# Second forms of three x blocks made in gate/up and kept in DRAM

## The chip, the cores and the metric

The kernel runs on 1 core of one Trainium2 chip. The metric is the device time of one execution in microseconds, the median of several runs; lower is better.

## The reference

With x of 2048 rows and 512 columns, all in float32:

```
g   = sigmoid((x * gate_w).sum(-1))
a   = real(DFT_seq(DFT_hidden(x)))       # as matmuls with cos and sin matrices
h   = silu(x @ w1) * (x @ w3)            # 512 -> 1376, "gate" and "up"
b   = h @ w2                             # 1376 -> 512
out = g * a + (1 - g) * b
```

The DFT along the sequence comes first in the kernel (matrices times x), then the one along the hidden axis.

## The kernel before, in words

**Arithmetic.** Each float32 operand is split in two parts of type float32r: a high part, a rounded copy that ScalarE makes (`high`, line 108), and a low part, the difference, that VectorE makes (`low`, line 111). A product of two operands is three matmuls (`mm3`, line 122: high x high, high x low, low x high), each of 128 x 128 by 512 columns. On top of that, products of 2 x 2 blocks are made with seven multiplications instead of eight, so each operand is needed as seven *forms*: blocks and sums of blocks. "First forms" are four of them, made from sums over the raw block (`sums1_here`, lines 168 and 170), "second forms" the other three (`sum2`, line 174, and `forms2`).

**Stages.** 1. Gate/up: 22 items (numbers 0 to 21), each a block of 128 columns of w1 and w3 and one half of the rows of x. From item 1 on each item of the main loop is a call of `gate_up(n)`: seven products of six matmuls, in the order X, Z, a product for item n + 3, X, Z, another for n + 3, X. X and Z are two PSUM banks that are read by ScalarE or VectorE between the products that are added to them. From item 19 on there is nothing left for later items, and an item has five products. 2. Streamed products: nine blocks, numbers 0 to 3 over the DFT matrices (`cc`), then over h and over the result so far. A block consists of steps; in blocks 0 to 3 a step has 12 matmuls, and there are 28 steps: seven forms by four pieces. The streamed operand is loaded, summed (lines 682 and 685) and split (`zo`) three steps ahead; the standing operand is x (blocks 0 to 3), in first forms A1 (steps 0 to 15) and second forms A2 (steps 16 to 27).

**What is made in gate/up besides.** In items 9, 11, 13 and 15 a block of w2 is loaded, summed and split; its low halves are queued early in items 10, 12, 14 and 16, and its forms are stored to DRAM (`w2sp`, lines 568 and 571). In items 12, 14, 16, 17, 18, 19 and 20 a block of x (`xr`, loaded by `load_a`, line 578, 512 KB) is made into its first forms, the eighth block in item 21. The first forms stand in pool `a1`, which has eight places less one and fills up block by block; the pool takes the place of the first x operand of gate/up once item 11 is done.

**What sets the order.** The schedule is written by hand. Each engine takes its instructions in program order and waits at the first one that is not ready. The lists `early`, `ahead`, `second`, `mid` and `at_end` hold functions that `gate_up(n)` runs at five places between its products. In `gate_up`, the copy of X (line 369) comes before `early`; the copy of Z (line 373, ScalarE) comes after `ahead`; the addition of X (line 382, VectorE) comes after `second`. SP issues all loads in program order: in an item first `wb` (1 MB, the weights' second forms, from DRAM, from item 13 on) for the next item, then `ws` (raw weights) for four items on, whose split is `wa`, then what stands in the lists. POOL issues all stores in program order: two of h in each item (256 KB each), and w2's. The raw buffers (`wide`) rotate in the order in which they are freed, so that a load can wait for one.

**Second forms before.** In block 0, all eight x blocks are loaded again (`load_a2`, line 738, steps 4 to 11), and from step 7 on summed and split (`make_a2`), one block a step.

Of the kernel before, what the change touches and what calls it, by code (L numbers as in the profile page):

```python
# [7 lines left out]
F32 = mybir.dt.float32  # L8
F32R = mybir.dt.float32r
# [3 lines left out]
P = 128  # L13
# [8 lines left out]
NG = NST // 2  # L22
# [4 lines left out]
K = 9  # L27
W2_AT = (9, 11, 13, 15)
A1_AT = (12, 14, 16, 17, 18, 19, 20)


@with_exitstack
def fnet_swiglu_gate_kernel(
# [20 lines left out]
    nc = tc.nc  # L54

    def pool(name, bufs, side, space=None):
        kw = {} if space is None else {"space": space}
        cm = tc.tile_pool(name=name, bufs=bufs, side=side, reuse_waits="tile", **kw)
        return cm, cm.__enter__()
# [6 lines left out]
    dram = ctx.enter_context(tc.tile_pool(name="dram", bufs=1, space=bass.MemoryType.DRAM))  # L66
# [29 lines left out]
    def wide(name):  # L96
        return take(F4, [P, 1024], F32, name)
# [4 lines left out]
    def free(*tiles):  # L102
        for t in tiles:
            _, places, at = HELD.pop(id(t))
            places.append(at)

    def high(hi, src):
        nc.scalar.activation(hi, src, AF.Copy)  # L108

    def low(hi, lo, src):  # L110
        nc.vector.tensor_sub(lo, src, hi.bitcast(F32))  # L111

    def split(hi, lo, src):
        high(hi, src)
        low(hi, lo, src)
# [16 lines left out]
    gs = dram.tile([NTB, 1, 512], F32, tag="gs", name="gs")  # L132
    gsp, ngsp = (dram.tile([2, P, 1024], F32, tag=k, name=k) for k in ("gsp", "ngsp"))
    dsp = [dram.tile([KD, P, 2, n, 256], F32, tag=f"dsp{n}", name=f"dsp{n}") for n in (4, 3)]
    w2sp = [dram.tile([NP2, P, 2, n, 256], F32, tag=f"w2sp{n}", name=f"w2sp{n}") for n in (4, 3)]
    wbsp = dram.tile([NC, P, 2, 4, 256], F32, tag="wbsp", name="wbsp")
    zsp = dram.tile([4 * NTB * P, 1024], F32, tag="zsp", name="zsp")
# [3 lines left out]
    def flat(ap):  # L141
        return ap.rearrange("p a n -> p (a n)")
# [22 lines left out]
    def sums1_here(r):  # L165

        a21, a11, a12, a22 = (r[:, i * 256 : (i + 1) * 256] for i in range(4))
        nc.vector.tensor_sub(a22, a22, a21)
        for d, v, w in ((a21, a22, a11), (a12, a12, a21)):
            nc.vector.scalar_tensor_tensor(d, v, -1.0, w, op0=ALU.mult, op1=ALU.subtract)  # L170

    def sum2(r):

        nc.vector.tensor_sub(r[:, :256], r[:, 256:512], r[:, :256])

    def forms2(r, t2):

        r = r.rearrange("p (a n) -> p a n", a=4)
        split(flat(t2[:, 0, 0:2]), flat(t2[:, 1, 0:2]), flat(r[:, 2:4]))
        split(t2[:, 0, 2], t2[:, 1, 2], r[:, 0])  # L180
# [8 lines left out]
    NI = len(ITEMS)  # L189
# [149 lines left out]
    early, ahead, second, mid, at_end = {}, {}, {}, {}, {}  # L339
# [177 lines left out]
    def do(work, n, f, *a):  # L517
        work.setdefault(n, []).append(lambda: f(*a))
# [55 lines left out]
    A1, A2, XR = [], [], {}  # L574
# [13 lines left out]
    def low_a(p):  # L588
        low(*parts_a1(p))
        free(XR.pop(p))  # L590

    for n in range(NI):
        if n in W2_AT:
            p = W2_AT.index(n)
            do(at_end, n - 1, load_w2, p)
            do(early, n, sums_w2, p)
            do(mid, n, high_w2, p)
            do(early, n + 1, low_w2, p)
        if n in A1_AT:
            p = A1_AT.index(n)  # L600
            do(at_end, n - 1, load_a, p)
            do(early, n, lambda p=p: sums1_here(XR[p]))
            do(mid, n, high_a, p)
            do(early, n + 1, low_a, p)

# [4 lines left out]
    n = NI - 1 - LOOK  # L610
    do(at_end, n - 1, F4.extend, [(f4_a, f"f4_{k}") for k in range(4, 5 + LOOK)])
    for k in range(LOOK + 2):
        do(at_end, n - 1 + k, lambda k=k: load_c(k))
    do(at_end, NI - 2, load_a, NG - 1)
    do(early, NI - 1, lambda: sums1_here(XR[NG - 1]))
    do(mid, NI - 1, lambda: split_c(0))
# [38 lines left out]
    def block(blk, k, q):  # L655
        if KIND[blk] == "F":
            return cc[blk, ("B11", "B12", "B22", "B21").index(k), q]
        if KIND[blk] == "H":
            return hsp[blk - NTB, ("B11", "B12", "B21", "B22").index(k), q]
        return z_rows(2 * (blk - NTB - 2) + (k in ("B12", "B22")), 2 * (k in ("B21", "B22")) + q)  # L660

    def cols(blk, q, form):

        return 512 if KIND[blk] == "H" and q == NQ[blk] - 1 and form in ("B21", "B22", "T4") else 1024
# [38 lines left out]
    def load_c(m):  # L703
        while LOADS and LOADS[0][0] <= m and F4:
            _, blk, k, q = LOADS.pop(0)
            r = RAW[blk, k, q] = wide(f"{k}_{blk}_{q}")
            n = cols(blk, q, k)
            nc.sync.dma_start(r[:, :n], block(blk, k, q)[:, :n])
# [6 lines left out]
    for n in range(1, NI):  # L715
        gate_up(n)
        if ITEMS[n] == (NC - 1, 0):
            close(xo0_cm)
            a1_cm, a1 = pool("a1", 1, "left")
# [4 lines left out]
    a2_cm, a2 = pool("a2", 1, "right")  # L724
    ut_cm, ut = pool("ut", 1, "right")
    F4[:0] = [(f4_b, f"f4_{k}") for k in range(5 + LOOK, 13)]
    ZO[:0] = [(zo_b, f"zo_{k}") for k in range(2, 4)]
    def load_a2(p):


        if p < NG // 2:
            t = a2.tile([P, 2, 3, 256], F32, tag=f"a2_{p + NG // 2}", name=f"xs{p}")
            XR[p] = t.rearrange("p h a n -> p (h a n)")[:, :1024]
        elif p < NG - 2:
            XR[p] = flat(ut.tile([P, 2, 512], F32, tag=("u3", "c21")[p % 2], name=f"xs{p}"))
        else:
            XR[p] = wide(f"xs{p}")
        nc.sync.dma_start(XR[p], xn[p])

    def make_a2(p):  # L740
        A2.append(a2.tile([P, 2, 3, 256], F32R, tag=f"a2_{p}", name=f"a2_{p}"))
        r = XR.pop(p)
        forms2(r, A2[p])
        if p >= NG - 2:
            free(r)

# [199 lines left out]
    def at(blk, n, f, *a):  # L946
        todo.setdefault(START[blk] + n, []).append((f, a))

    at(1, 1, load_score, 1)
    for p in range(NG):  # L950
        at(0, 4 + p, load_a2, p)

        at(0, 7 + p, lambda p=p: sum2(XR[p]))
    for p in range(NG):
        at(0, 8 + p, make_a2, p)

    at(0, 0, lambda: nc.scalar.activation(act0, act0, AF.Sigmoid))
# [3 lines left out]
    for i, (src, sp, p) in enumerate(late):  # L961
        blk, b = 1 + i // 2, i % 2
        n = (17, 24)[b]
# [11 lines left out]
    for p in range(KD):  # L975
        early = p < NG - NP2
# [76 lines left out]
```

## Time and profile before

| | |
|---|---|
| median of 3 runs | 679.55 us (678.91 to 679.66) |
| the profiled execution: time, span | 679.73 us, 678.0 us |
| VectorE busy | 602.1 us |
| ScalarE busy | 366.9 us |
| HBM read, written | 114.82 MB, 57.16 MB |

In the rows, PE is TensorE, PEld its weight loads, DVE VectorE, ACT ScalarE, POOL GpSimd and SPq SyncE's DMA issues; q0 is the queue of POOL's transfers and q1 that of SP's. A row of a timeline gives start and length in us, engine, line, operation, what is written from what, shape and count; in brackets the idle time before it and what ended it. A row of the windows gives the stretch and its length, then busy us and instruction count of PE, PEld, DVE, ACT and POOL, the granted TensorE clock, the DMA share and GB/s. A row of the transfers gives size and us from issue to landing. The matmuls overlap, so the time from one to the next is read from starts, not from lengths. The clock was 1.00 throughout.

### The profile page before, as it was taken

To read this page: it belongs to the slowest core of one execution; us is meant where nothing else is said; L and a number is where in the kernel's file an instruction comes from. 1 tells how busy PE (TensorE), PEld (TensorE's weight loads), DVE (VectorE), ACT (ScalarE), POOL (GpSimd) and SP (SyncE) were. 2 spreads that over 40 slices of the span, in tenths; PEclk is the share of its full clock that TensorE was granted. 3 is DMA by queue.
4 is the path that set the end of the run, shared out by engine and by line. 5 is a ranking of instruction groups with operands and counts; after the bars stand their busy time and mean duration, and the time that the engine had idled before them with its cause. 6 is when DMAs were issued, how large, how long until landed. Compare 5 with 4: busy or idle time off the path is not lost.

```text
span 678.0 us, 8627 instructions
## 1 busy us (share of the span) xinstructions
PE 671.2 (99%) x3089; PEld 581.8 (86%) x3089; DVE 602.1 (89%) x737; ACT 366.9 (54%) x480; POOL 64.0 (9%) x118
## 2 busy tenths in 40 slices
PE   9999999999999999999999999999999999999997
PEld 6888888888888888888888888888888888888886
DVE  6999988787679999987999799979998897898996
ACT  6675566655446764464554554554546455445452
POOL 0011112121110000000110001100110000000000
PEclk9999999999999999999999999999999999999999
DMA  7585557499998656912497328915999982874942
GB/s 294 205 306 218 218 196 277 187 328 388 410 418 289 254 177 230 352 63 93 156 378 288 94 88 334 385 56 208 360 420 419 414 281 91 310 281 154 330 135 93
DMA packets 45547, 172.54 MB, mean 255 GB/s; under 512 B 5312, under 2 KB 5696, under 8 KB 41664
## 3 DMA queue, kind: packets, MB, share of 16 engines
q1 hardware_dynamic: 32608, 118.63, 48.2%
q0 software_dynamic: 12608, 52.97, 19.6%
q8 instruction: 24, 0.39, 0.2%
q10 hardware_dynamic: 288, 0.39, 0.2%
q14 instruction: 19, 0.16, 0.1%
HBM read 114.82 MB, written 57.16 MB: 254 GB/s over the span
## 4 chain that ended last, share of the span: by engine, by line
PE 51%; issue 37%; DMA 6%; DVE 3%; POOL 3%; ACT 0%; SPq 0%; POOLq 0%; DVEq 0%; ACTq 0%
PE P L122 24%; PE X L122 15%; PE Z L122 8%; PE Y L122 3%; DMA B<-hsp 2%; DMA dsp<-late_0l 2%; DMA xs_B<-xt 1%; POOL zsp L821 1%; DMA p5g<-gs 1%; POOL dsp L803 1%; POOL w2sp L803 1%; DVE wa L111 1%; DVE xs_B L214 1%; DVE zo L111 0%; DVE xo L111 0%
## 5 line engine op out<-in xcount | busy, mean ns | idle before, releaser
L122 PE MATMUL P<-zo,a 128*128 128x512 f32 x1344 | 290.9, 379 | 1.0 <-DVE zo L111 1.0
L122 PEld LDWEIGHTS P<-zo,a 128*128 128x128 f32 x1344 | 253.7, 189 | 38.0 <-DVE zo L111 2.0
L108 ACT ACTIVATE zo<-B 128x1024 fp32r<-128x1024 f32 (+1 forms) x182 | 188.4, 1041 | 180.2 <-DVE B L682 83.5
L111 DVE TENSOR_TENSOR zo<-B,zo 128x1024 fp32r<-128x1024 f32 (+1 forms) x182 | 217.2, 1201 | 30.9 <-ACT zo L108 30.2
L122 PE MATMUL P<-zo,H 128*128 128x512 f32 x468 | 101.4, 379 | 0.1
L122 PEld LDWEIGHTS P<-zo,H 128*128 128x128 f32 x468 | 88.4, 189 | 13.0 <-DVE zo L111 0.5
L682 DVE TENSOR_TENSOR B<-B,B 128x1024 f32<-128x1024 f32 (+1 forms) x78 | 92.7, 1188 | 1.2 <-DMA B<-hsp 1.1
L122 PE MATMUL X<-xo,wb 128*128 128x512 f32 x378 | 89.2, 380 | 0.2 <-DVE xo L111 0.2
L122 PEld LDWEIGHTS X<-xo,wb 128*128 128x128 f32 x378 | 71.1, 189 | 11.3 <-DVE xo L111 0.6
L122 PE MATMUL P<-zo,Y 128*128 128x512 f32 x336 | 72.7, 379 | 0.0
L122 PEld LDWEIGHTS P<-zo,Y 128*128 128x128 f32 x336 | 63.5, 189 | 9.0
L334 POOL DMA_DIRECT2D hsp<-h x42 | 23.0, 548 | 121.0 <-DVE h L388 67.7
L685 DVE TENSOR_TENSOR B<-B,B 128x1024 f32<-128x1024 f32 x26 | 31.6, 1217 | 0.0
L122 PE MATMUL X<-xo,wa 128*128 128x512 f32 x126 | 31.0, 381 | 0.1
L122 PE MATMUL Y<-xo,wa 128*128 128x512 f32 x126 | 30.6, 379 | 0.0
L122 PE MATMUL Z<-xo,wb 128*128 128x512 f32 x126 | 30.6, 379 | 0.0
L122 PE MATMUL Z<-xo,wa 128*128 128x512 f32 x126 | 30.6, 379 | 0.0
L913 ACT ACTIVATE zu<-P 128x512 f32<-128x512 f32 x32 | 19.0, 595 | 17.3 <-PE P L122 15.7
L111 DVE TENSOR_TENSOR wa<-ws,wa 128x768 fp32r<-128x768 f32 (+1 forms) x22 | 19.3, 880 | 9.6 <-ACT wa L108 9.5
L122 PEld LDWEIGHTS X<-xo,wa 128*128 128x128 f32 x126 | 23.5, 189 | 4.4 <-DVE wa L111 0.5
L122 PEld LDWEIGHTS Y<-xo,wa 128*128 128x128 f32 x126 | 23.8, 189 | 3.4
L122 PEld LDWEIGHTS Z<-xo,wb 128*128 128x128 f32 x126 | 23.8, 189 | 3.4
(137 smaller groups left out, 544.3 us busy)
## 6 DMA issues: line engine op xcount, KB each, us to landing
B<-cc SPq DMA_DIRECT2D x64, 512.0 KB, 6.4
hsp<-h POOLq DMA_DIRECT2D x42, 256.0 KB, 3.8
B<-hsp SPq DMA_DIRECT2D x20, 512.0 KB, 10.9
wbsp<-wb POOLq DMA_DIRECT2D x8, 1024.0 KB, 4.3
wb<-wbsp SPq DMA_DIRECT2D x8, 1024.0 KB, 8.3
B<-zsp SPq DMA_DIRECT2D x16, 512.0 KB, 8.2
H<-w2sp SPq DMA_DIRECT2D x6, 1024.0 KB, 9.4
ws<-w SPq DMA_DIRECT2D x11, 512.0 KB, 4.8
```

The costliest lines, as they stand in the source:

```text
L108: nc.scalar.activation(hi, src, AF.Copy)
L111: nc.vector.tensor_sub(lo, src, hi.bitcast(F32))
L122: nc.tensor.matmul(ps.rearrange("p (n a) -> p n a", a=2), u, turns(v), **kw)
L214: nc.vector.tensor_sub(t, *(ST[g, v] for v in SUMS[k]))
L334: nc.gpsimd.dma_start(hsp[g, b + k, j // 2, :, j % 2 * 512 : (j % 2 + 1) * 512], h)
L682: nc.vector.tensor_add(t, t, RAW[blk, b, q][:, :n])
L685: nc.vector.tensor_sub(t, RAW[blk, "B12", q], t)
L803: nc.gpsimd.dma_start(flat(dst[:, k]), v[:, : 1024 - 256 * j].bitcast(F32))
L821: return nc.gpsimd.dma_start(z_rows(blk, k), flat(t))
L913: nc.scalar.activation(U[name][:, r], ps[r], AF.Copy)
```

## The change

The second forms of x blocks 0, 1 and 2 are made in gate/up, in items 12, 14 and 16, from the raw block that is there for the first forms. They are made in places of pool `a1` whose own block comes later (numbers 6, 5 and 4), and stored to a new DRAM tensor `a2sp` (768 KB for each block). `high_a2` stands in `early`: one subtraction on VectorE and two high halves on ScalarE; `low_a2` stands in `ahead`: two low halves, the store, and then the sums for the first forms, which stood in `early` before. In block 0, the three blocks are loaded in finished form, and their sums and splits fall away. The raw x blocks 3 to 6 are loaded one item earlier, and the first streamed blocks (`load_c`) one item later, except that the last two come in the same item.

```diff
+NE = 3
...
+    a2sp = dram.tile([NE, P, 2, 3, 256], F32, tag="a2sp", name="a2sp")
...
+    A2E = {}
+
+    def parts_a2(p):
+        t = A2E[p]
+        return [(flat(t[:, 0, i:j]), flat(t[:, 1, i:j]), v) for i, j, v in
+                ((0, 2, XR[p][:, 512:]), (2, 3, t[:, 0, 3].bitcast(F32)))]
+
+    def high_a2(p):
+        k = NG - 2 - p
+        A2E[p] = a1.tile([P, 2, 4, 256], F32R, tag=f"a1_{k}", name=f"a2e_{p}")
+        nc.vector.tensor_sub(A2E[p][:, 0, 3].bitcast(F32), XR[p][:, 256:512], XR[p][:, :256])
+        for v in parts_a2(p):
+            high(*v[::2])
+
+    def low_a2(p):
+        for v in parts_a2(p):
+            low(*v)
+        nc.gpsimd.dma_start(a2sp[p], A2E.pop(p)[:, :, :3].bitcast(F32))
+        sums1_here(XR[p])
...
         if n in A1_AT:
             p = A1_AT.index(n)
-            do(at_end, n - 1, load_a, p)
-            do(early, n, lambda p=p: sums1_here(XR[p]))
+            do(at_end, n - (1 if p < NE else 2), load_a, p)
+            if p < NE:
+                do(early, n, high_a2, p)
+                do(ahead, n, low_a2, p)
+            else:
+                do(early, n, lambda p=p: sums1_here(XR[p]))
...
     for k in range(LOOK + 2):
-        do(at_end, n - 1 + k, lambda k=k: load_c(k))
+        do(at_end, min(n + k, NI - 1), lambda k=k: load_c(k))
...
+    def new_a2(p):
+        A2.append(a2.tile([P, 2, 3, 256], F32R, tag=f"a2_{p}", name=f"a2_{p}"))
+        return A2[p]
     def load_a2(p):
+        if p < NE:
+            nc.sync.dma_start(new_a2(p).bitcast(F32), a2sp[p])
+            return
...
     for p in range(NG):
         at(0, 4 + p, load_a2, p)
-        at(0, 7 + p, lambda p=p: sum2(XR[p]))
-    for p in range(NG):
+        if p >= NE:
+            at(0, 7 + p, lambda p=p: sum2(XR[p]))
+    for p in range(NE, NG):
         at(0, 8 + p, make_a2, p)
```

More of the change, by code (lines that the diff above doesn't have):

```diff
@@ L740, in make_a2 @@
     def make_a2(p):
-        A2.append(a2.tile([P, 2, 3, 256], F32R, tag=f"a2_{p}", name=f"a2_{p}"))
         r = XR.pop(p)
-        forms2(r, A2[p])
+        forms2(r, new_a2(p))
         if p >= NG - 2:
```

## The prediction

> **What bounds the kernel now.** I read the page first, then the chain of waits, then TensorE's timeline.
>
> ```profile
> span 678.0 us, 8627 instructions
> PE 671.2 (99%) x3089; PEld 581.8 (86%) x3089; DVE 602.1 (89%) x737; ACT 366.9 (54%) x480; POOL 64.0 (9%) x118
> ...
> 508.24 165.83 PE P L122 x767
> ```
>
> The last line is the tail of the chain: 767 matmuls in a row in 165.83 us, 0.216 us each. The change alters no matmul, so it can only fill or open gaps in this beat. TensorE's timeline has two places with gaps near the edit. The first is block 0 of the streamed products, where the second forms of x are first used (step 16 on):
>
> ```profile
> 208.26 44.48 PE L122 MATMUL P<-zo,a 128*128 128x512 f32 x205
> 253.42 2.86 PE L122 MATMUL P<-zo,a 128*128 128x512 f32 x12 [0.69 <-DVE zo L111]
> 256.63 18.61 PE L122 MATMUL P<-zo,a 128*128 128x512 f32 x85 [0.35 <-DVE zo L111]
> ```
>
> From 208.26 to 256.63 is 48.37 us for 217 matmuls; at 0.216 they need 46.87, so 1.5 us is lost, and the rows name VectorE's low halves (L111). The windows say why:
>
> ```profile
> 228.00:238.00 10.00, 10.00 (x48) 8.77 (x47) 10.00 (x15) 8.22 (x14) 0.00 (x0) 1.00 0.40 142
> 238.00:248.00 10.00, 10.00 (x48) 8.74 (x48) 10.00 (x17) 6.93 (x12) 0.00 (x0) 1.00 0.55 174
> 248.00:258.00 10.00, 8.96 (x40) 7.10 (x39) 9.93 (x13) 5.39 (x7) 0.00 (x0) 1.00 0.73 234
> ```
>
> Third figure: VectorE busy 10.00, 10.00 and 9.93 of 10 us, while TensorE (first figure) falls to 8.96. VectorE is late, nothing else. DMA (last two figures: share, GB/s) is slack. The second place is gate/up item 18:
>
> ```profile
> 177.81 2.93 PE L122 MATMUL X<-xo,wb 128*128 128x512 f32 x12
> 180.57 1.46 PE L122 MATMUL Z<-xo,wb 128*128 128x512 f32 x6
> 182.17 1.64 PE L122 MATMUL X<-xo,wa 128*128 128x512 f32 x6
> ```
>
> Starts should be 2.59 and 1.30 apart; they are 2.76 and 1.60, so about 0.5 us is lost, on wb and on wa just loaded.
>
> **Part 1, block 0: what is removed.** For three of eight x blocks the sum (L174) and two low halves leave VectorE:
>
> ```profile
> 233.02 0.42 DVE L174 TENSOR_TENSOR xs<-xs 128x256 f32<-128x256 f32 x1
> 233.35 1.02 DVE L111 TENSOR_TENSOR a<-xs,a 128x512 fp32r<-128x512 f32 x2
> 234.29 1.22 DVE L111 TENSOR_TENSOR zo<-B,zo 128x1024 fp32r<-128x1024 f32 x1
> ```
>
> From start to start a block costs 0.33 + 0.94 = 1.27 us, three cost 3.8 us, all ahead of the steps that are late by 1.5. I take the whole 1.5 as gained. What could be late next is the sum B12-B11 (L685), which has the same queue and comes earlier by the same amount. ScalarE's six high halves leave too; it was not full (6.93 of 10). SP loads 768 KB in place of 512 KB, three times, in steps 4 to 6, for use at step 16:
>
> ```profile
> xs<-xn SPq DMA_DIRECT2D x8, 512.0 KB, 12.2
> ```
>
> Landing within 12.2 us, or half as much more, against 10 steps of 2.6 us costs nothing; without that cover each would stop TensorE outright.
>
> **Part 2, gate/up: what is added.** Items 12, 14 and 16 get, per block, one 256-wide subtraction, two low halves (together 1.27 us of VectorE), two high halves on ScalarE and a 768 KB store on POOL's queue. These three items are just those in which VectorE also splits a w2 block, and the subtraction is queued behind those low halves. On ScalarE the 256-wide high half waits for it, and behind that stands the copy of Z (L373), which must be done before TensorE adds the next product to Z. So the added wait holds ScalarE, the Z copy, and then TensorE. In item 14:
>
> ```profile
> 142.84 0.84 ACT L108 ACTIVATE wa<-ws 128x768 fp32r<-128x768 f32 x1 [1.92 <-DMA ws<-w]
> 143.72 0.96 DVE L111 TENSOR_TENSOR wa<-ws,wa 128x768 fp32r<-128x768 f32 x1 [1.21 <-ACT wa L108]
> 147.33 0.42 DVE L168 TENSOR_TENSOR xr<-xr 128x256 f32<-128x256 f32 x1
> 145.64 0.60 ACT L373 ACTIVATE u<-Z 128x512 f32<-128x512 f32 x1 [0.46 <-PE Z L122]
> 148.03 1.46 PE L122 MATMUL Z<-xo,wa 128*128 128x512 f32 x6
> ...
> 235.88 0.42 ACT L108 ACTIVATE a<-xs 128x256 fp32r<-128x256 f32 x1 [0.34 <-DVE xs L174]
> ```
>
> The L168 row is where VectorE is done with w2 and where the subtraction will stand. From there: 0.42 (subtraction) + 0.42 (high half, last row) + 0.60 (Z copy) = 1.44 us until TensorE may go on with Z. In item 14 that is 148.77, against 148.03.
>
> Item 12: here the copy is in time (128.30 + 1.44 = 129.74; Z's next product starts two products, 2.59, before the 132.49 below, at 129.90), but VectorE has 1.27 us more to do before it adds X (L382), and X's last product must wait for that:
>
> ```profile
> 128.30 0.41 DVE L168 TENSOR_TENSOR xr<-xr 128x256 f32<-128x256 f32 x1
> 131.01 0.68 DVE L382 TENSOR_TENSOR u<-u,X 128x512 f32<-128x512 f32 x1
> 132.49 2.75 PE L122 MATMUL X<-xo,wb 128*128 128x512 f32 x12
> ```
>
> 131.01 + 1.27 + 0.68 = 132.96 against 132.49. First term: +0.5.
>
> **Part 3, the transfers.** The stores go into a stretch in which DMA is full:
>
> ```profile
> 142.60:151.70 9.10, 9.10 (x44) 7.95 (x44) 7.63 (x14) 5.43 (x8) 2.39 (x5) 1.00 0.91 304
> 151.70:160.80 9.10, 9.10 (x44) 7.97 (x43) 6.79 (x11) 4.88 (x9) 1.13 (x3) 1.00 1.01 418
> 169.80:178.90 9.10, 9.10 (x44) 7.94 (x43) 6.74 (x11) 3.85 (x6) 1.42 (x3) 1.00 1.01 405
> ...
> w2sp<-w2b POOLq DMA_DIRECT2D x4, 768.0 KB, 9.0
> ```
>
> Shares of 1.01; the only slack is 0.09 of 9.10 us, 0.8 us, in item 14. A store of 768 KB (0.786 MB; the w2b store has the same size and queue) takes 1.88 us at 418 GB/s. How much of it the loads lose depends on how the queues share:
>
> ```profile
> q1 hardware_dynamic: 214, 1.17, 71.0%
> q0 software_dynamic: 147, 0.47, 29.2%
> ...
> q0 software_dynamic: 341, 2.00, 95.5%
> q1 hardware_dynamic: 38, 0.11, 6.6%
> ```
>
> The first pair is 156 to 160 us, the second 168 to 173, when POOL's stores (q0) took nearly everything. The bounds are 0 and 1.88 us of delay per store. I take two thirds, 1.2 us: the store goes ahead of loads as in the second pair, but part of what it takes is room of the h stores queued behind it on POOL. The Trainium skill ("DMA: Bandwidth & Descriptors", Queues, rings and completion order) says each DMA engine takes turns between its queues, packet by packet. By that rule, estimated, a load beside a store would lose half of the store's time. The second pair does not agree with equal turns, though it does not show how much was ready on q1.
>
> On POOL the two stores of h stand behind the added one:
>
> ```profile
> hsp<-h POOLq DMA_DIRECT2D x42, 256.0 KB, 3.8
> ```
>
> Their buffer is written again about one item (9 us) after the second of them is issued. Landing in twice 3.8 plus 1.88 stays just within that, so I count 0; past it ScalarE's copy of X would wait, with the Z copy behind it.
>
> Item 14, with wa 1.2 us later: VectorE comes to its subtraction at 148.53, the Z copy ends at 149.97, TensorE is there at 148.03 + 0.5 = 148.53. Second term: +1.4, together 1.9.
>
> Item 16:
>
> ```profile
> 161.60 0.84 ACT L108 ACTIVATE wa<-ws 128x768 fp32r<-128x768 f32 x1 [2.25 <-DMA ws<-w]
> 166.10 0.42 DVE L168 TENSOR_TENSOR xr<-xr 128x256 f32<-128x256 f32 x1
> 166.16 1.46 PE L122 MATMUL Z<-xo,wa 128*128 128x512 f32 x6
> ```
>
> Its wa again waits for its load. That load is issued with TensorE's pace, 1.9 later; the queue is 2 x 1.2 - 0.8 = 1.6 later; I take the larger. 166.10 + 1.9 + 1.44 = 169.44 against 166.16 + 1.9 = 168.06. Third term: +1.4, together 3.3.
>
> Item 18 has no slack for its loads. Three stores less the slack are 2.8 us; one x block that SP now issues an item earlier (xr, 512 KB, 1.25 us at 418) comes on top: 4.0, against 3.3 of slip. That block can go into the queue only when a buffer of the w2 block is free, perhaps behind the others, so I count none of the difference, and the 0.5 us of before stays. The first streamed blocks go behind the x loads and keep their order among themselves:
>
> ```profile
> 174.99 0.45 SPq L708 DMA_DIRECT2D B<-cc  x1
> 205.06 2.00 ACT L108 ACTIVATE zo<-B 128x1024 fp32r<-128x1024 f32 x2
> ```
>
> The first of them is issued 30 us before its split on ScalarE; an item later is 9 us, so I count 0. It would cost directly if load and queue together took more than the remaining 21 us.
>
> **Sum.** +0.5 + 1.4 + 1.4 - 1.5 = +1.8. The profiled execution took 679.73 us with its span of 678.0; 679.73 + 1.8 = 681.5. The median shown, 679.55, lies 0.18 lower, so I predict 681.4. The span should be about 679.8. The rivals' times stand on the median.
>
> **Rivals.** A measurement of this kernel can tell some 0.2%, 1.4 us, from no change: 678.2 to 680.9.
>
> *Faster: the cover holds.* If ScalarE's copies and the loads keep their places, only block 0 is seen: -1.5, and up to another 0.5 if item 18 gains: 678.0 to 677.5. For it: VectorE is busy 7.63 and 6.79 of 9.10 in these items, so the work itself has room. Against: the order of the queues, 147.33 + 1.44 against 148.03.
>
> *No load delayed.* Then item 12 costs 0.5; item 14 148.77 - 148.53 = 0.2; item 16 166.10 + 1.44 = 167.54 against 166.16 + 0.7 = 166.86, 0.7; and item 18 gains its 0.5. +0.9 - 1.5 = -0.6: 679.0. For it the 71% of the loads in the first pair; against it shares of 1.01.
>
> *Equal turns.* Each store takes half of 1.88 from the loads, 0.94. Item 14: 147.33 + 0.94 + 1.44 = 149.71 against 148.53, 1.2; item 16 slips by 1.7 and loses 1.4; item 18 gains most of its 0.5, as 3 x 0.94 - 0.8 = 2.0 of queue is less than the slip of 3.1. 0.5 + 1.2 + 1.4 - 0.4 - 1.5 = +1.2: 680.8. For it the first pair, in which neither queue is shut out; against it the second. This is how the rule of the Trainium skill named above would have it.
>
> *The stores delay in full.* 3 x 1.88 - 0.8 + 1.25 = 6.1 us at item 18, whatever went before, since it has no slack: 6.1 - 1.5 = +4.6, 684.1. It decides from the point at which the third store precedes wb and ws of item 17.
>
> *No gain in block 0*, if a load or ScalarE is late in VectorE's place: +3.3, 682.9. Against it: DMA shares of 0.40 to 0.73 there.
>
> **Chances.** Forecast 0.40, full delay 0.14, no gain in block 0 0.07: slower 0.61. Equal turns 0.12, no load delayed 0.10: same 0.22. Cover holds: 0.17. The range 678.0 to 684.5 reaches from the faster rival's upper value to past the full delay; it leaves out about half of the faster case and the worst of the slowest, some 0.15. Within slower alone it is 680.9 to 684.5.
>
> **What would show it.** In the changed profile: TensorE's rows at 253 and 256 us without waits on zo; a low half (L111) and ScalarE waiting for the subtraction in items 12, 14 and 16; gaps before Z<-xo,wa in items 14 and 16, of 1.4 us each, named after the Z copy (L373 now); a gap of 0.5 before the last X product of item 12; ws taking longer from issue to landing than before. The forecast is wrong if items 14 and 16 keep the beat (then the time is under 679), if the gaps are at wb or wa instead (DMA alone, over 683), or if step 16 of block 0 still waits.

## The result: 0.6% slower, and the profile after

The changed kernel takes 683.26 us (median of 6 runs, 682.6 to 684.06) against 679.55 us: ratio 1.0057, 95% interval 1.0046 to 1.0068, or +3.7 us. The forecast was 681.4, in a range of 678.0 to 684.5. The profiled execution took 683.16 us with a span of 681.4. Its clock was 1.00, as before.

Block 0 first. TensorE's timeline of the changed kernel, and its windows (busy us of PE, PEld, DVE, ACT, POOL, then clock, DMA share and GB/s):

```profile
213.22 72.05 PE L123 MATMUL P<-zo,a 128*128 128x512 f32 x333
```

```profile
228.00:238.00 10.00, 10.00 (x48) 8.77 (x47) 9.34 (x9) 6.93 (x9) 1.08 (x2) 1.00 0.83 322
238.00:248.00 10.00, 10.00 (x49) 8.74 (x48) 8.87 (x13) 7.50 (x13) 0.00 (x0) 1.00 0.64 217
248.00:258.00 10.00, 10.00 (x48) 8.77 (x47) 10.00 (x14) 4.78 (x7) 0.00 (x0) 1.00 0.58 165
```

All of block 0 is one row without a gap, and VectorE has room from 228 to 248 us. The 1.5 us are gained (1.6 measured). Gate/up, again TensorE's timeline, items 12, 14 and 16:

```profile
130.96 1.46 PE L123 MATMUL Y<-xo,wa 128*128 128x512 f32 x6
132.80 2.88 PE L123 MATMUL X<-xo,wb 128*128 128x512 f32 x12 [0.38 <-DVE u L384]
...
147.38 1.46 PE L123 MATMUL X<-xo,wb 128*128 128x512 f32 x6
150.26 1.56 PE L123 MATMUL Z<-xo,wa 128*128 128x512 f32 x6 [1.43 <-ACT u L375]
151.66 1.46 PE L123 MATMUL Y<-xo,wa 128*128 128x512 f32 x6
...
164.61 1.46 PE L123 MATMUL Z<-xo,wb 128*128 128x512 f32 x6
166.59 1.64 PE L123 MATMUL X<-xo,wa 128*128 128x512 f32 x6 [0.52 <-ACT h L401]
168.06 1.46 PE L123 MATMUL X<-xo,wb 128*128 128x512 f32 x6
171.11 1.56 PE L123 MATMUL Z<-xo,wa 128*128 128x512 f32 x6 [1.59 <-ACT u L375]
172.51 1.46 PE L123 MATMUL Y<-xo,wa 128*128 128x512 f32 x6
```

Six matmuls take 1.30 us from start to start. Item 12 loses 0.54 (1.84 instead of 1.30) and 0.1 behind it, before X; item 13, not among these rows, 0.2; item 14 loses 1.6 + 0.1, before Z; item 16 loses 0.85 before and in the product for item 19, and 1.75 + 0.1 before Z. From the first Z product of item 12 to the first product of block 0 it was 126.01 to 208.26, 82.25 us, and is 125.78 to 213.22, 87.44: +5.2. In the first 260 matmuls of block 0 it is -1.6. The rest (start and tail) differs by -0.2, which makes the 3.4 of the two spans.

The wait on Z is the predicted one. ScalarE and VectorE in item 16 of the changed kernel:

```profile
165.21 0.84 ACT L109 ACTIVATE wa<-ws 128x768 fp32r<-128x768 f32 x1 [4.35 <-DMA ws<-w]
167.43 0.63 ACT L109 ACTIVATE a2e<-xr 128x512 fp32r<-128x512 f32 x1
170.15 0.42 ACT L109 ACTIVATE a2e<-a2e 128x256 fp32r<-128x256 f32 x1 [2.10 <-DVE a2e L605]
170.48 0.58 ACT L375 ACTIVATE u<-Z 128x512 f32<-128x512 f32 x1
```

```profile
168.77 1.02 DVE L112 TENSOR_TENSOR w2b<-w2r,w2b 128x512 fp32r<-128x512 f32 x2
169.71 0.42 DVE L605 TENSOR_TENSOR a2e<-xr 128x256 f32<-128x256 f32 x1
```

ScalarE stands 2.10 us before the second high half, for a subtraction (L605) that VectorE does behind w2's low halves; the copy of Z (L375) comes after it, at 170.48, and Z's next product at 171.11. The first row shows the other half of the matter: ScalarE had stood 4.35 us for `ws`, whose split began at 161.60 before.

### The profile page after: what moved, and what is told of

It is laid out like the page before. It is cut to its first block, busy times and chain, and to the rows that moved or that the text cites. A ratio compares the mean times of both kernels' runs of the same rounds, so it can differ in the third digit from the quotient of the medians.

```text
span 681.4 us, 8632 instructions
## 1 busy us (share of the span) xinstructions
PE 671.4 (99%) x3089; PEld 581.5 (85%) x3089; DVE 602.3 (88%) x737; ACT 366.7 (54%) x480; POOL 66.0 (10%) x121
## 4 chain that ended last, share of the span: by engine, by line
PE 81%; DMA 9%; DVE 6%; issue 1%; ACT 1%; SPq 0%; POOL 0%; DVEq 0%; ACTq 0%; POOLq 0%
PE P L123 62%; PE X L123 11%; PE Z L123 6%; DMA ws<-w 4%; PE Y L123 3%; DMA B<-hsp 2%; DMA dsp<-late_0l 2%; DMA xs_B<-xt 1%; DVE wa L112 1%; DVE zo L112 1%; DVE w2a L112 1%; DVE xs_B L216 1%; DVE w2b L112 0%; ACT wa L109 0%; DVE xo L112 0%
## 5 line engine op out<-in xcount | busy, mean ns | idle before, releaser
L123 PEld LDWEIGHTS Z<-xo,wa 128*128 128x128 f32 x126 | 23.6, 189 | 7.1 <-ACT u L375 3.8
```

What stands on the lines that cost most here:

```text
L123: nc.tensor.matmul(ps.rearrange("p (n a) -> p n a", a=2), u, turns(v), **kw)
```

## The experiments

My theory had three causes in gate/up, namely the order on ScalarE, VectorE's 1.27 us in item 12, and the store traffic that makes `ws` late, and a gain in block 0 that has nothing to do with them. The rivals were the traffic alone, with the order harmless, and VectorE's added work alone. The two last columns give the two stretches, measured as above in the profiled execution of each kernel (differences to before, in us). The kernel before was run again with each set and took 679.50 to 679.76 us there; each ratio is to its own set.

| kernel | median us | ratio, 95% interval | profiled us | gate/up | block 0 |
|---|---|---|---|---|---|
| the change | 683.26 | 1.0057 (1.0046 to 1.0068) | 683.16 | +5.2 | -1.6 |
| forms made, not stored | 681.23 | 1.0022 (1.0012 to 1.0031) | 681.56 | +1.5 | 0.0 |
| the same, subtraction first | 681.15 | 1.0027 (1.0014 to 1.0039) | 681.25 | +1.0 | 0.0 |
| store only | 682.48 | 1.0044 (1.0028 to 1.0061) | 681.85 | +1.9 | 0.0 |
| store only, doubled | 687.23 | 1.0107 (1.0091 to 1.0122) | 688.16 | +8.5 | 0.0 |
| the change, subtraction first | 683.18 | 1.0046 (1.0031 to 1.0061) | 681.31 | +3.2 | -1.6 |
| block 0 only | 678.48 | 0.9982 (0.9973 to 0.9991) | 678.14 | -0.2 | -1.6 |
| order of loads only | 679.27 | 0.9996 (0.9988 to 1.0005) | 679.38 | -0.2 | 0.0 |
| order mended, three blocks | 682.75 | 1.0043 (1.0029 to 1.0057) | 682.82 | +4.7 | -1.6 |
| order mended, two blocks | 680.69 | 1.0020 (1.0011 to 1.0029) | 680.20 | +1.8 | -1.6 |
| order mended, one block | 680.76 | 1.0023 (1.0012 to 1.0034) | 680.83 | +2.3 | -1.3 |
| late places | 677.73 | 0.9976 (0.9966 to 0.9986) | 677.64 | -0.4 | -1.6 |
| late places, loads of before | 679.65 | 1.0008 (0.9998 to 1.0018) | 681.68 | +3.8 | -1.6 |

Where the profiled time lies far from the median, the median weighs more than the two last columns: "the change, subtraction first" was traced 1.9 us below its median, "late places, loads of before" 2.0 and "store only, doubled" 0.9 us above theirs.

**Forms made, not stored.** Block 0 is as before.

```diff
-        nc.gpsimd.dma_start(a2sp[p], A2E.pop(p)[:, :, :3].bitcast(F32))
+        A2E.pop(p)
```

> The changed gate/up with its loads, but the finished forms are not stored; block 0 loads and makes all eight x blocks as before. If the order of the queues costs the time (ScalarE's Z copy behind the subtraction) and the stores only add to it: item 12 loses 0.6, item 14 0.2 to 0.4 and item 16 0.7 us, the 0.5 of item 18 may go: 680.0 to 681.2. If the stores' traffic alone costs it: 679.6, as before. If VectorE's added work costs it wherever it stands: 3 x 1.27, 683.

Measured: 681.23 us, at the upper end. The waits sit where the order puts them, item 12 as in the change and item 16 before Z:

```profile
165.80 1.46 PE L123 MATMUL X<-xo,wb 128*128 128x512 f32 x6
168.24 1.56 PE L123 MATMUL Z<-xo,wa 128*128 128x512 f32 x6 [0.98 <-ACT u L375]
```

Item 14 loses nothing. Items 12, 13 and 16 lose 2.1 us together, and some 0.6 of item 18's old loss falls away. So without the stores the added work and its order cost 1.5 us, not 5.2. The rival "VectorE's work alone" is out, as it would have taken 683 us, and so is "the traffic alone", which would have left 679.6.

**Store only.** The kernel before, with w2's second forms stored once more in items 12, 14 and 16.

```diff
         nc.gpsimd.dma_start(w2sp[1][p], W2R[p][3][:, :, :3].bitcast(F32))
+        if p:
+            nc.gpsimd.dma_start(a2sp[p - 1], W2R[p][3][:, :, :3].bitcast(F32))
```

> The kernel before with one more 768 KB store on POOL's queue behind w2's stores in items 12, 14 and 16 (w2's second forms a second time, to memory that nobody reads); nothing else. If the stores delay wb and ws in full, item 18, which has no slack, loses what the queue is late, some 3 us, with wa waits in items 14 and 16 before it: 682 to 683.5. If the order of the queues is the cause and loads give way little: 679.6 to 680.5.

Measured: 682.48 us. No engine computes anything more, and the kernel is 2.7 us slower (682.48 - 679.76, the kernel before in the same runs). What TensorE's weight loads waited for, items 12 to 21:

```profile
PEld X L122 <- DMA wb<-wbsp: 1.4, 1, 1.4
PEld X L122 <- ACT h L400: 1.4, 3, 0.7
PEld X L122 <- DVE wa L111: 0.6, 3, 0.2
```

The first is `wb`, straight from DMA; the other two stand behind the split of `wa`, which waits for `ws` (ScalarE's copy L400 is queued behind it). By the medians the traffic alone costs more than the work alone. The edit has one side effect: the added store reads `w2b`'s buffer, and in item 15 ScalarE waits until that is done (0.72 us for w2's own store before).

```profile
161.46 0.94 ACT L108 ACTIVATE w2b<-w2r 128x512 fp32r<-128x512 f32 x2 [3.25 <-DMA a2sp<-w2b]
163.17 0.84 ACT L108 ACTIVATE wa<-ws 128x768 fp32r<-128x768 f32 x1 [0.77 <-DMA ws<-w]
```

After that wait ScalarE stands another 0.77 us for `ws`, so it is the late `ws`, and not the buffer, that sets when `wa` is split.

**Store doubled.** Two such stores in each of the three items.

```diff
+            for k in (0, 3):
+                nc.gpsimd.dma_start(a2sp[p - 1 + k], W2R[p][3][:, :, :3].bitcast(F32))
```

> As the run with one added store in items 12, 14 and 16, but with two in each. If loads are delayed in proportion once the slack is used up, each of three more stores costs 1.5 to 1.9 us: 686.5 to 688. If the loads are served in turns and the stores wait in their own queue: 683 to 684.5.

Measured: 687.23 us, 4.75 more than with one. That is 1.6 us for each of the three further stores (1.4 by the two ratios), as the forecast in proportion had it; the 683 to 684.5 forecast for loads served in turns are out.

**Subtraction first**, with the stores and without them.

```diff
-                do(early, n, high_a2, p)
+                early.setdefault(n, []).insert(0, lambda p=p: high_a2(p))
```

> The changed kernel with the subtraction and the high halves queued ahead of w2's low halves, so that ScalarE's Z copy does not wait for them. If the order costs the time: the two waits before Z in items 14 and 16 (1.6 and 1.75 us) go, VectorE's addition of X is late by some 0.6 in items 12, 14 and 16: 680.5 to 681.5. If the queue of transfers is the bound, the same time is lost at wa in items 16 and 18 instead: 682.5 to 683.3.

> As the run with the forms made and not stored, but with the subtraction and the high halves ahead of w2's low halves. Without the stores' traffic the order alone is on trial: the wait before Z in item 16 (1.25 us) goes, 0.85 in items 12 and 13 stays, VectorE's addition of X may cost 0.3 in 16: 679.8 to 680.4, against 681.2 with the order of the change. If the order doesn't matter: 681.2.

Measured: 683.18 us with the stores, 681.15 without, against 683.26 and 681.23 with the order of the change. By the ratios the new order saves 0.7 us with the stores, give or take 1.3, and costs 0.3 without them, give or take 1.1. The forecasts for the case that the order costs the time, 680.5 to 681.5 and 679.8 to 680.4, are both missed. The wait before Z does go in both, but part of it comes back elsewhere. Without the stores, 1.2 us before Z in item 16 became 0.6 before X. With the stores, weight loads of items 12 to 21 waited as follows:

```profile
PEld X L123 <- DVE u L384: 3.0, 3, 1.2
PEld X L123 <- DMA wb<-wbsp: 0.7, 1, 0.7
PEld X L123 <- DVE wa L112: 0.5, 2, 0.3
PEld X L123 <- ACT h L401: 0.5, 1, 0.5
...
```

No row, nor the last one of 0.2 us left out here, has the copy of Z any more (3.8 us in the change); VectorE's addition of X (L384) has 3.0 us instead of 0.8, and `wb` has come in. In this one execution, 681.31 us, gate/up is still 2.0 us shorter than in the change; the other three of this kernel took 682.87 to 683.71, and where they lose it no trace shows. So by the medians the order is not worth what my theory gave it; that it is worth something less is not excluded.

**Block 0 only.** Gate/up of before; the second forms of the three x blocks are not made at all, and block 0 loads w2's second forms, of the same size, in their place.

```diff
+            nc.sync.dma_start(new_a2(p).bitcast(F32), w2sp[1][p])
```

> Gate/up of before; block 0 of the changed kernel, in which the three finished blocks are loaded from w2's second forms of the same size (so the sequence transform is made with wrong numbers for these). If the 1.5 us in block 0 come from VectorE's three sums and splits: 677.9 to 678.2. If something else is late in their place: 679 to 679.6.

Measured: 678.48 us, -1.3 against the 679.76 of the same runs, and in the profile -1.6 in block 0. The gain is there, and it is all that the change has to give; the forecast for it, 677.9 to 678.2, was 0.3 too low.

**Order of loads only.**

```diff
-            do(at_end, n - 1, load_a, p)
+            do(at_end, n - (1 if p < 3 else 2), load_a, p)
...
-        do(at_end, n - 1 + k, lambda k=k: load_c(k))
+        do(at_end, min(n + k, NI - 1), lambda k=k: load_c(k))
```

> The kernel before with the change's order of loads alone (x blocks 3 to 6 an item earlier, first streamed blocks an item later). I expect no change, 679.3 to 680.1. If the x block that now goes ahead of wb and ws of item 17 (512 KB, 1.25 us) delays them, item 18, which has no slack: 680.5 to 681.

Measured: 679.27 us, no change.

**Order mended, with three, two and one block.** Subtraction and high halves first; low halves, store and sums behind the addition of X; loads as before.

```diff
+                early.setdefault(n, []).insert(0, lambda p=p: high_a2(p))
+                do(mid, n, low_a2, p)
...
-            do(mid, n, high_a, p)
+            do(at_end if p < NE else mid, n, high_a, p)
```

> Three blocks; the subtraction and high halves ahead of w2's low halves, the low halves, the store and the sums for the first forms behind the addition of X, the high half of the first forms at the item's end; loads in the order of before. If the transfers are the bound and the order only decides where the delay shows: the loss of the store alone (2.5 us of gaps in gate/up), less 1.6 in block 0: 680 to 681. If the order is the bound: 678 to 678.6.

> The same with two blocks, in items 12 and 14: 2.5 of the 3.8 us leave VectorE, still more than the 1.5 that it is late. By transfers: one store less ahead of item 17's loads, 1.5 to 1.9 us less loss than with three, 678.4 to 679.5. By order: as with three, 678 to 678.6.

> The same with one block, in item 12, whose store meets the emptiest stretch. 1.27 us leave VectorE of the 1.5 that it is late. By transfers: the store's 1.9 us are largely absorbed by the 0.8 us of slack in item 14 and the slack of the loads there, 678.2 to 678.9. By order: 678.4 to 678.6 as well; a loss against before would speak for a cost of the store that does not depend on where it stands.

Measured: 682.75, 680.69 and 680.76 us; all slower than forecast by either theory. My edit has a fault of its own, in all three: in item 12 VectorE's work now stands ahead of the low half of `wa`, and item 13 pays 1.4 us (three blocks):

```profile
136.25 0.59 PE L123 MATMUL X<-xo,wa 128*128 128x512 f32 x2
137.44 1.13 PE L123 MATMUL X<-xo,wa 128*128 128x512 f32 x4 [0.60 <-DVE wa L112]
138.81 1.56 PE L123 MATMUL X<-xo,wb 128*128 128x512 f32 x6 [0.23 <-ACT h L371]
```

So these runs say little on the order. They do say that the third block, in item 16, costs most, its store and its work together: 2 us between three blocks and two, nothing that can be told between two and one.

**Late places.** Instead of blocks 0 to 2, blocks 3 and 4 are made, in items 17 and 18, which split no w2 block, behind the addition of X; the stores go out one item later. Block 0 loads these two finished. Once with the change's order of loads, once with that of before.

```diff
+EARLY2 = (3, 4)
+PLACE2 = (5, 6)
...
+            if p in EARLY2:
+                do(mid, n, make_early2, p)
+                do(early, n + 1, store_early2, p)
```

> The kernel before with the change's order of loads, and the second forms of two other x blocks (3 and 4) made in items 17 and 18, where no w2 block is split, all of it behind the addition of X; the stores go out one item later, after the loads of wb and ws that have no slack. 2.5 us leave VectorE in block 0, which is late by 1.6. If the loss of the change comes from where its stores and its wait stand: the gain of block 0 is kept, 677.9 to 678.7. If 768 KB more in the full stretch cost time wherever they stand: 679.5 to 681.

> The same with the order of loads of before. The x blocks then come about 9 us later, but they are not waited for ahead of the addition of X: 677.9 to 678.9; by the other theory 679.5 to 681.

Measured: 677.73 us with the change's order of loads, faster than the kernel before by 0.24% (ratio 0.9976, 0.9966 to 0.9986), and the quickest of all; 679.65 with the old one, above the 677.9 to 678.9 that I expected. Windows of the first, gate/up and block 0:

```profile
178.90:188.20 9.30, 9.30 (x45) 8.15 (x44) 7.96 (x14) 5.77 (x10) 1.77 (x3) 1.00 1.01 402
238.00:248.00 10.00, 10.00 (x48) 8.77 (x47) 10.00 (x15) 6.47 (x11) 0.00 (x0) 1.00 0.92 331
248.00:258.00 10.00, 10.00 (x48) 8.77 (x47) 9.93 (x13) 4.97 (x5) 0.00 (x0) 1.00 0.97 338
```

TensorE is full in all three. DMA is as full as before where the first store goes out (1.01), and still the stores cost nothing. I take two reasons for it: the loads behind them are not needed for a while, and the stretch from 198 to 208 us, with a DMA share of 0.81 before, had room (1.02 now). With the old order of loads the same stores delay the raw x blocks, and VectorE waits for these ahead of the addition of X, 3.9 us in two waits, in an execution of 681.68 us (by the medians the loss is 1.9):

```profile
DVE xr L171 <- DMA xr<-xn: 3.9, 2, 2.0
```

So the reordering of loads, which alone does nothing, is what lets stores stand here.

## Why the prediction was right, and by how much

Direction, range and places were right; of 3.7 us it had 1.8. Term by term, as forecast and measured in the profile:

- Block 0: -1.5, measured -1.6. Nothing came in VectorE's place.
- Item 12, VectorE ahead of the addition of X: +0.5, measured +0.65. Not forecast: 0.2 us in item 13 on `wa`, which VectorE now reaches later.
- Item 14, ScalarE held before the Z copy: +1.4, measured +1.7. `ws` was 1.5 us later (its split began at 144.36 instead of 142.84), not 1.2: it was issued 0.4 later and took 9.5 us to land instead of 8.4.
- Item 16: +1.4, measured +2.7. **This is the step that failed.** I took the larger of the slip of the issue and the delay of the queue, 1.9 us. They add: `ws` was issued 2.34 us later (154.82 instead of 152.48) and took 10.3 us to land instead of 9.0, together 3.6 us. Issue and landing, before and then in the change:

```profile
152.48 0.68 SPq L231 DMA_DIRECT2D ws<-w  x1
ws<-w SPq DMA_DIRECT2D x1, 384.0 KB, 9.0
...
154.82 1.13 SPq L233 DMA_DIRECT2D ws<-w  x1
ws<-w SPq DMA_DIRECT2D x1, 384.0 KB, 10.3
```

The split began at 165.21 instead of 161.60. That makes 0.85 us before the product for item 19, a wait that the forecast did not have, and then the Z copy on top.
- Item 18: 0, measured -0.1. The queue was 5.0 us late by then (the split of the last `ws` began at 185.76 instead of 180.79), but TensorE had slipped as far.

The forecast came out low, and one sign set for its being wrong came in part: the time is over 683, and there is a gap at `wa` (0.85 us), though beside the waits before Z and not in their place.

The price of a store, 1.2 us, held for the first three: alone they cost 2.7 us, which with the 0.8 us of slack makes about 1.2 for each. The next three cost 1.6 each, nearer the full 1.88. The 0 for the stores of h was luck in part: the 3.8 us taken for one is the median over the whole kernel, but in the full stretch the two issued from 149 to 156 us took 8.0 on the median before, and the one there in the change took 11.1. No copy of X waits for them in the change; with the doubled stores one did, for 2.2 us.

On the rule of turns that the prediction weighed (the Trainium skill, "DMA: Bandwidth & Descriptors", Queues, rings and completion order): the prediction took turns for equal time, which gave 680.8, and equal time is not what the traces show. From 130 to 134 us of the kernel before (packets, MB, share of the 16 engines):

```profile
q0 software_dynamic: 139, 0.97, 67.6%
q1 hardware_dynamic: 133, 0.48, 29.4%
```

The two queues moved nearly as many packets, so turns packet by packet may well be there; but a packet of the stores was 7.0 KB on average and one of the loads 3.6, and the stores took over twice the time.

What stayed wrong in the reasoning is the weight given to the order. The forecast put 2.8 us down to ScalarE's wait. The wait is in the trace just there, but two runs with it removed are no quicker by their medians. In item 14 the term hung on the late `ws`, since without the stores nothing is lost there; in item 16 it did so only in part, since 1.2 us stay without them. Behind each stood another wait: with the order changed, 1.1 and 0.8 us came back at the addition of X, in the one execution traced. How the 5.2 us split between traffic and work can't be said as a sum: alone they cost 2.7 and 1.5 us by medians (682.48 - 679.76, 681.23 - 679.76), together, by 683.26 - 679.55 and the 1.3 of block 0, 5.0. The remaining 0.8 I take for their meeting, a late `ws` on an engine with less room; that was argued, not shown.

## What to carry to other kernels

Before moving work to an earlier stage because an engine has room there, look at what the move sends through the queues: here the engines had room and DMA, at a share of 1.01, had none. Where DMA is full, look at which transfer is next behind the new one: here a store of 768 KB cost up to 1.6 of its 1.88 us ahead of a load without slack, and two such stores cost nothing ahead of loads that could wait, while the same two with the old order of loads cost 1.9. When a wait in the trace has a name, take it away in one run before calling it the cause, since the next one may stand right behind it.

## What the runs showed that I had not expected

A load order that changes nothing by itself (ratio 0.9996) made the difference of 1.9 us once stores were added (679.65 against 677.73). And the time for added stores is steep: three cost 2.7 us, six 7.7 (687.23 - 679.57). I take it that the slack that the first ones use up is gone for the others; no run shows that by itself.
